# Fused attention and feed-forward on one core: weight loads issued back to back, a norm moved to another engine, and two groups of small steps re-timed

## The chip, the cores and the metric

The kernel runs on one NeuronCore of one Trainium2 chip. The metric is the device time of one execution in microseconds (us), as the median of several runs; lower is better. The profile is one execution taken by the hardware profiler; its span (279.4 us before the change) is about 2 us shorter than the measured time (281.28 us). Every run quoted is fast, with a granted TensorE clock of 0.997 to 1.0, unless the text says otherwise.

Engine names in the profile: PE is TensorE (matmuls), PEld its weight loads, DVE is VectorE, ACT is ScalarE, POOL is GpSimd, SP is SyncE. An added q (POOLq, SPq, PEq) is that engine's queue or sequencer.

## The reference, cut to what matters

For 8 batches, 8 heads, 576 tokens and head size 64, the first half is an attention without a score matrix: Q is normalised over the head size, K over the tokens, and K-transposed times V is a 64 by 64 matrix per head. The second half is a feed-forward layer on 4608 tokens of width 512, with 2048 hidden units and a swish that has its own `beta` per hidden unit.

```python
q_s = exp(q - max_d(q));  q_s = q_s / (sum_d(q_s) + 1e-9)
k_s = exp(k - max_s(k));  k_s = k_s / (sum_s(k_s) + 1e-9)
kv  = einsum('bhsd,bhse->bhde', k_s, v)
x   = einsum('bhsd,bhde->bhse', q_s, kv)      # then reshaped to [4608, 512]
h   = x @ w_in                                # [4608, 2048]
g   = h * sigmoid(beta * h)
out = g @ w_out                               # [4608, 512]
```

## The kernel before

The kernel works through nine slabs. Slabs 0 to 7 hold the first 512 tokens of batches 0 to 7; slab 8 holds the 64 tokens left over of each batch. Each slab has two passes on TensorE. Pass 1 is 64 matmuls of `x @ w_in` (16 tiles of 4), each tile followed by a Silu on ScalarE and a scaling on VectorE. Pass 2 is the product with `w_out`. From slab 1 on it is done with sums of quarters, seven products in place of eight, for which VectorE makes the sums (`GS`, `WSUM`). The attention of the next batch is threaded into the matmuls of the slab before it or of its own slab: small steps get a tick number, and one tick is one matmul of pass 1 (32/56 of a tick in the fast pass 2).

The attention of one batch has these steps: `exp` of Q and K on ScalarE; row-sum and reciprocal of the norm on VectorE; the norm's multiply on VectorE or GpSimd; a transpose of Q to `QT` (on TensorE in the first batches, by DMA later); a cast of V to `VB`; K-V products; a scaling by VectorE (`KVD`); an output product and its copy to `XT`, which is what pass 1 reads. Each group covers two heads, and there are four groups (`hp` 0 to 3) to a batch.

Each engine runs its own instructions in program order. Compute instructions on GpSimd are made to wait for one another by the scheduler. And the weights are loaded by DMAs that GpSimd issues (they also change float32 to bf16 on the way), so a DMA can only be issued when GpSimd gets to it in its program.

```python
def norm_main(b, hp0, n, eng=DVE):
    ...
    add(DVE, lambda e: e.tensor_reduce(s_, a, AX.X, ALU.add), r=ks, w=[("qs", i, hp0)])
    add(DVE, lambda e: e.reciprocal(v_, s_), r=[("qs", i, hp0)], w=[("qi", i, hp0)])
    add(eng, lambda e: e.tensor_tensor(a, a, vb, ALU.mult), r=ks + [("qi", i, hp0)], w=ks)
...
def norm_turn(b, hp0):            # norm of two groups, multiply on GpSimd, transpose by DMA
    norm_main(b, hp0, 2, POOL)
    turn(b, hp0, 2)
...
# the head of the program
norm_main(0, 0, 1, DVE)
norm_main(0, 1, 1, POOL)
load_win(0, 512, 0, 2)            # first piece of WIN, 256 KB in SBUF
norm_main(0, 2, 1, DVE)
cast_vr_s(0)                      # cast of the 64 left-over rows of V, on GpSimd
norm_main(0, 3, 1, POOL)
load_win(0, 512, 2, 4)            # second piece, 256 KB
for c0 in range(512, DFF, 512):
    load_win(c0, c0 + 512)        # third to fifth piece, 512 KB each
for c in range(4):
    load_wout(c)                  # four pieces of WOUT, 512 KB each
...
# batch 1, issued in slab 0: its queries are loaded once WOUT's first piece has landed
load_main("qf", qt_h, QF, 1, split=4, after=P.writer[("wout", 3, 0)])
...
w_sum(0, 0, 4); w_sum(2, 0, 4)
norm_main(1, 0, 1, DVE)
norm_main(1, 1, 1, POOL)
cast_vr_s(1)
w_sum(0, 4, 4); w_sum(2, 4, 4)
norm_main(1, 2, 1, DVE)
norm_main(1, 3, 1, DVE)
...
# slab 3: batch 3's last two output steps; pass 1 starts with 3 tiles, all of m = 0 first,
# then m = 1, m = 2, m = 3, where matmul m reads XT[m]
todo += [(1, steps(out_step, 3, 2)), (2.5, steps(out_step, 3, 3, MB, ACTE))]
...
# slabs 4 to 6: K-V products of batch b spread over ticks 8 to 36
s = spread(kv_steps(b, (0, 1)) + kv_steps(b, (2, 3)), 8, 36)
```

(The pieces stand in the order of the program; cuts are marked by three dots, and the comments are mine.)

The softmax here doesn't subtract the row's maximum and nothing guards it: scores larger than these inputs give would overflow.

Of the kernel before, what the change touches and what calls it, by code (L numbers as in the profile page):

```python
# [41 lines left out]
class Program:  # L42
# [12 lines left out]
    def add(self, eng, fn, r=(), w=(), bank=(), slot=None, after=(), war=False):  # L55
        op = Op(eng, fn, slot)
        op.pos = len(self.ops)
        deps = op.deps
        deps.extend(after)
        for k in r:  # L60
            deps.extend(self.writer.get(k, ()))
            self.readers.setdefault(k, []).append(op)
        for k in w:
            for d in self.readers.get(k, ()):
                if d is not op and (war or not self._same(d, op)):
                    deps.append(d)
            for d in self.writer.get(k, ()):
                if not self._same(d, op):
                    deps.append(d)
            self.readers[k] = []  # L70
            self.writer[k] = [op]
        for k in bank:
            t = self.touch.setdefault(k, {})
            for e, d in t.items():
                if e != eng:
                    deps.append(d)
            t[eng] = op
        if eng == POOL and slot is None:
            if self.pool is not None:
                deps.append(self.pool)  # L80
            self.pool = op
        self.ops.append(op)
        return op
# [71 lines left out]
def bass_efficient_attn_shen__then__act_swish_beta_kernel(  # L155
# [12 lines left out]
    with ExitStack() as es:  # L168
# [50 lines left out]
        MB = (5, 6, 7)  # L219

        P = Program()
        add = P.add
# [101 lines left out]
        def norm_main(b, hp0, n, eng=DVE):  # L324
            i = b % 2
            a = bass.AP(EQ[i], hp0 * 512, [[2048, 128], [64, 8 * n], [1, 64]])
            s_ = bass.AP(QS[i], hp0 * 8, [[32, 128], [1, 8 * n]])
            v_ = bass.AP(QI[i], hp0 * 8, [[32, 128], [1, 8 * n]])
            vb = bass.AP(QI[i], hp0 * 8, [[32, 128], [1, 8 * n], [0, 64]])
            ks = [("eq", i, hp) for hp in range(hp0, hp0 + n)]  # L330
            add(DVE, lambda e: e.tensor_reduce(s_, a, AX.X, ALU.add), r=ks, w=[("qs", i, hp0)])  # L331
            add(DVE, lambda e: e.reciprocal(v_, s_), r=[("qs", i, hp0)], w=[("qi", i, hp0)])  # L332
            add(eng, lambda e: e.tensor_tensor(a, a, vb, ALU.mult), r=ks + [("qi", i, hp0)],  # L333
                w=ks)
# [13 lines left out]
            add(eng, lambda e: (e.copy if eng == ACTE else e.tensor_copy)(o, a),  # L348
                r=[("vf", i, hp), ("vone", i)], w=[("vb", i, hp)], after=after)

        def cast_vr_s(b):
            o = bass.AP(VRS[b], 0, [[NHP * VW, 128], [VW, NHP], [1, 128]])
            a = bass.AP(VRF, 0, [[512, 128], [128, NHP], [1, 128]])
            add(POOL, lambda e: e.tensor_copy(o, a), r=[("vrf", 0), ("vrf", 1)], w=[("vrs", b)])

        def cast_vr(b, hs=(0, 1), after=()):
            pi = (b // 2) % 2
# [66 lines left out]
        def kv_steps(b, hps, pool=MB):  # L424
            i = b % 2
            st = {}

            def one(n, hp, j):
                if n == 0 and j == 0:
                    st["b"] = bank(pool)  # L430
                bk = st["b"]
                l, r_, ke, kv, ko = kv_rows(b, hp, j)
                mm(PS[bk][:, 256 * n:256 * n + 129], l, r_[:, 0:129], j == 0, j == 4,
                   r=ke + kv, w=[("ps", bk)], bk=bk)
                if n == len(hps) - 1 and j == 4:
                    c, k_ = hps[0], len(hps)
                    s_ = bass.AP(PS[bk], 128, [[512, 128], [256, k_]])
                    add(DVE, lambda e: e.reciprocal(RC[i][:, c:c + k_], s_),
                        r=[("ps", bk)], w=[("rc", i, h2) for h2 in hps], bank=[bk])
                    for m, h2 in enumerate(hps):  # L440
                        kvd(b, h2, bk, 256 * m)
            return [lambda n=n, hp=hp, j=j: one(n, hp, j) for n, hp in enumerate(hps)
                    for j in range(5)]
# [54 lines left out]
            turn_rem()  # L498

        def attn(b):  # L500
            s = spread(kv_steps(b, (0, 1)) + kv_steps(b, (2, 3)), 8, 36)
            x = []
            for hp in range(NHP):
                x += out_step(b, hp, MB, ACTE if hp % 2 else DVE)
            s += spread(x, 84, 108)
            return s
# [17 lines left out]
        def spread(steps, lo, hi):  # L524
            return [(lo + (hi - lo) * k / len(steps), s) for k, s in enumerate(steps)]
# [50 lines left out]
        norm_main(0, 0, 1, DVE)  # L576
        norm_main(0, 1, 1, POOL)
        load_win(0, 512, 0, 2)
        norm_main(0, 2, 1, DVE)
        cast_vr_s(0)  # L580
        norm_main(0, 3, 1, POOL)
        load_win(0, 512, 2, 4)
        for c0 in range(512, DFF, 512):
            load_win(c0, c0 + 512)
# [2 lines left out]
        ones_s(1)  # L587
        ones(1)
        ones(0)
        exp_kr_s(0)  # L590
        cast_v(0, 0, DVE)
        go(t_steps(0, (0,), HEAD, ACTE))
        exp_k(0, 0, 1)
        warm(7, 0)
        go(t_steps(0, (1,), HEAD, ACTE))
        exp_k(0, 1, 1)
        cast_v(0, 1, DVE)
        warm(4, 0)
        go(t_steps(0, (2,), HEAD, ACTE))
        exp_k(0, 2, 1)  # L600
        cast_v(0, 2, DVE)
        go(kv_steps(0, (0,), HEAD))
        warm(3, 0)
        go(t_steps(0, (3,), HEAD, ACTE))
        exp_k(0, 3, 1)
        go(kv_steps(0, (1,), HEAD))
        cast_v(0, 3, DVE)
        warm(2, 0)
        go(out_step(0, 0, HEAD, ACTE))
        go(kv_steps(0, (2,), HEAD))  # L610
        go(out_step(0, 1, HEAD, ACTE))
# [225 lines left out]
        for t in range(NSLAB):  # L837
            todo = []
            if t == 0:
                todo = [(x, steps(t_steps, 1, (hp,), NOW, ACTE))  # L840
                        for hp, x in enumerate((97, 106, 114, 119))]
                todo += [(107, one(exp_kr_s, 1))]
                todo += [(x, one(exp_k, 1, hp, 1)) for hp, x in enumerate((108, 115, 120, 125.5))]
                todo += [(x, one(cast_v, 1, hp, DVE if hp else POOL))
                         for hp, x in enumerate((115, 118.5, 123, 127))]
                todo += [(x, steps(kv_steps, 1, (hp,), NOW))
                         for hp, x in enumerate((118, 122, 126))]
                todo += [(x, steps(out_step, 1, hp, NOW, ACTE)) for hp, x in enumerate((121, 125))]
                todo += [(117, one(o2_evac, 0, 0, 3, ACTE))]
                todo += [(2, steps(out_step, 0, 3, HEAD, DVE))]  # L850
            elif t < 4:
                todo = attn_late(t + 1)
                if t == 3:
                    todo += [(1, steps(out_step, 3, 2)), (2.5, steps(out_step, 3, 3, MB, ACTE))]
                if t == 1:
                    todo += [(1, steps(out_step, 1, 2, (3,), ACTE)),
                             (3, steps(kv_steps, 1, (3,), (7,))),
                             (6, steps(out_step, 1, 3, (7,), DVE)),
                             (6.1, one(w_diff, 0)), (6.2, one(w_diff, 1))]
            elif t < 7:  # L860
                todo = attn(t + 1)
                if t > 3:
                    todo += spread(outr_steps(2 * t - 5), *((72, 88), (40, 56), (60, 76))[t - 4])
            elif t == 7:
                todo = spread(outr_steps(1), 32, 48)
# [74 lines left out]
            if t == 1:  # L940
                on(0, exps, 2)
                on(0, casts, 2)
                on(0, load, 4)
                on(2, norm_main, 2, 0, 2, POOL)
                on(3, norm_main, 2, 2, 2, POOL)
                on(3, g_diff, 0)
            elif t == 2:
                on(0, exps, 3)
                on(2, norm_turn, 3, 0)
                on(3, norm_turn, 3, 2)  # L950
                on(3, g_diff, 0)
                on(3, load, 5)
                on(4, exp_q, 4)
                on(4, casts, 4)
                on(6, norm_turn, 4, 0)
                on(7, norm_turn, 4, 2)
            elif t == 3:
                on(0, exp_k, 4)
                on(0, exp_kr, 4)
                on(0, exp_q, 5)  # L960
                on(3, g_diff, 0)
                on(4, norm_turn, 5, 0)
                on(5, norm_turn, 5, 2)
                on(4, exp_qr)
                on(5, exp_k, 5)
                on(5, norm_turn_rem)
                on(5, casts, 5)
                on(5, load, 6)
                on(7, load_rem, "qrf", qt_h, QRF, 4)
            elif t + 2 < B:  # L970
                b = t + 2
                on(0, exps, b)
                on(0, casts, b)
                if t == 4:
                    on(0, load, 7)
                on(3, norm_turn, b, 0)
                on(4, norm_turn, b, 2)
# [40 lines left out]
```

## Time and profile before

| | |
|---|---|
| time | 281.28 us (281.21 to 281.29, 3 runs) |
| span of the profiled run | 279.4 us |
| TensorE busy | 269.5 us, 96% |
| granted TensorE clock | 0.998 |

TensorE is busy 96% of the span, so a change to the other engines can only win what TensorE spends waiting. This is the line of the profile page with busy time, share of the span and number of instructions of each engine.

```profile
PE 269.5 (96%) x1844; PEld 167.7 (60%) x1844; DVE 192.6 (69%) x413; ACT 182.7 (65%) x285; POOL 65.2 (23%) x84
```

The view of waits for the kernel before tells who TensorE waited for. The columns are: engine and line of what waited, the engine and line (or DMA) that released it, then the idle us in total, the number of waits, and the longest one.

```profile
PE PS L376 <- DMA WIN<-in_moe_w_in_dram: 1.5, 2, 1.0
PE PS L376 <- POOL VB L348: 1.3, 1, 1.3
PE PS L376 <- DVE XT L456: 1.3, 1, 1.3
PE PS L376 <- DVE WARM L225: 1.2, 1, 1.2
```

The last of these is the start of the program. The other three are three separate places in time.

**The head.** The timeline of GpSimd before the change; the columns are start, us from the first start to the last end, engine, line, operation, output and input, count, and in brackets the idle time ahead.

```profile
9.40 0.95 POOL L551 DMA_DIRECT2D WIN<-in_moe_w_in_dram  x1
10.36 0.64 POOL L354 CAST VRS<-VRF 128x512 bf16<-128x512 f32 x1
11.08 1.10 POOL L333 TENSOR_TENSOR EQ<-EQ,QI 128x512 bf16<-128x512 bf16 x1
12.14 3.06 POOL L551 DMA_DIRECT2D WIN<-in_moe_w_in_dram  x4
15.16 2.99 POOL L557 DMA_DIRECT2D WOUT<-in_moe_w_out_dram  x4
```

A cast and a multiply stand between the first WIN issue and the other four. TensorE's timeline of the same kernel shows what comes of that: it starts on WIN at 14.87, stops at 16.61 for the second piece, and at 19.94 for the third.

```profile
15.58 1.03 PE L376 MATMUL PS<-XT,WIN 128*128 128x512 bf16 x4
17.61 2.33 PE L376 MATMUL PS<-XT,WIN 128*128 128x512 bf16 x10 [1.00 <-DMA WIN<-in_moe_w_in_dram]
20.42 10.53 PE L376 MATMUL PS<-XT,WIN 128*128 128x512 bf16 x48 [0.48 <-DMA WIN<-in_moe_w_in_dram]
```

The view of windows gives each engine's busy time (and number of instructions) for each microsecond; the last three columns are the granted clock, the DMA engines' busy share (it can exceed 1) and the GB/s that they moved.

```profile
15.00:16.00 1.00, 1.00 (x6) 0.31 (x4) 0.52 (x2) 0.91 (x2) 1.00 (x3) 1.00 0.79 85
16.00:17.00 1.00, 0.61 (x3) 0.10 (x1) 0.47 (x1) 0.99 (x2) 1.00 (x2) 1.00 0.89 127
```

From 18 us on the same column reads about 205 GB/s. So there is a hole in the weight stream just while TensorE waits for weights.

**Slab 3.** The timeline around 108 us, before the change: VectorE's row-sum and reciprocal for batch 4 are ahead of the third XT copy of batch 3, and TensorE stops for that copy.

```profile
107.41 1.21 DVE L331 TENSOR_REDUCE QS<-EQ 128x16 f32<-128x1024 bf16 x1
107.42 0.81 PE L376 MATMUL PS<-XT,WIN 128*128 128x512 bf16 x3
108.65 0.25 DVE L332 RECIPROCAL QI<-QS 128x16 f32<-128x16 f32 x1
108.82 0.63 DVE L456 CAST XT<-PS 128x512 bf16<-128x512 f32 x1
109.51 1.68 PE L376 MATMUL PS<-XT,WIN 128*128 128x512 bf16 x7 [1.28 <-DVE XT L456]
```

**Slab 4.** After eight matmuls of pass 1 comes the first K-V product of batch 5, and its V cast on GpSimd is not done.

```profile
136.40 1.89 PE L376 MATMUL PS<-XT,WIN 128*128 128x512 bf16 x8
138.92 2.65 POOL L348 CAST VB<-VF 128x512 bf16<-128x512 f32 x4
139.59 0.23 PE L376 MATMUL PS<-VB,EK 128*128 128x129 bf16 x1 [1.30 <-POOL VB L348]
```

### The profile page before, as it was taken

How to read it: one execution, taken by the hardware profiler on the slowest of the kernel's cores; microseconds unless marked ns; L12 is line 12 of the kernel's file. 1: busy time of each engine (PE TensorE's matmuls, PEld its weight loads, DVE VectorE, ACT ScalarE, POOL GpSimd, SP SyncE). 2: the span in 40 equal slices, each digit the busy share in tenths (PEclk: the TensorE clock that was granted, in tenths of full speed). 3: DMA queues.
4: the chain of work that ended last, by engine and by line, in shares of the span. 5: the costliest groups of instructions: out<-in, count | busy, mean ns of one | idle time of the engine just before them, and what ended most of it. 6: DMA issues, size and time to landing. Idle time of an engine off the chain costs nothing.

```text
span 279.4 us, 4714 instructions
## 1 busy us (share of the span) xinstructions
PE 269.5 (96%) x1844; PEld 167.7 (60%) x1844; DVE 192.6 (69%) x413; ACT 182.7 (65%) x285; POOL 65.2 (23%) x84
## 2 busy tenths in 40 slices
PE   8979999999999998999899999999999999999994
PEld 3434444448754784468555885488548844874583
DVE  4944586787758797768749794969487649635862
ACT  4777658789478965886677946794674467018610
POOL 2791021006521089000720551035100100000000
PEclk9999999999999999999999999999999999999999
DMA  7999999999992029920389999202700130003005
GB/s 214 314 163 206 223 320 350 290 244 371 360 256 118 0 49 286 305 116 0 65 258 297 328 339 165 95 4 51 231 2 0 21 150 0 2 26 124 2 0 150
DMA packets 57253, 45.39 MB, mean 162 GB/s; under 512 B 26496, under 2 KB 56208, under 8 KB 56208
## 3 DMA queue, kind: packets, MB, share of 16 engines
q1 hardware_dynamic: 52368, 40.38, 50.9%
q0 software_dynamic: 4240, 4.19, 9.3%
q10 hardware_dynamic: 624, 0.53, 0.6%
q8 instruction: 14, 0.23, 0.3%
q14 instruction: 7, 0.06, 0.1%
HBM read 36.71 MB, written 9.44 MB: 165 GB/s over the span
## 4 chain that ended last, share of the span: by engine, by line
PE 81%; DVE 8%; POOL 5%; DMA 3%; issue 1%; ACT 0%; POOLq 0%
PE PS L376 53%; PE PS L727 28%; POOL EQ L333 3%; DMA WIN<-in_moe_w_in_dram 3%; DVE QS L331 2%; DVE GT L693 1%; POOL VB L348 1%; PE PS L374 1%; DVE XT L456 1%; DVE KVD L418 1%; DVE QI L332 1%; DVE O2S L775 1%; POOL VR L361 0%; POOL EQR L341 0%; POOL WIN L551 0%
## 5 line engine op out<-in xcount | busy, mean ns | idle before, releaser
L376 PE MATMUL PS<-XT,WIN 128*128 128x512 bf16 x576 | 131.5, 379 | 2.8 <-DMA WIN<-in_moe_w_in_dram 1.5
L627 ACT ACTIVATE GT<-PS,BETA 128x512 bf16<-128x512 f32 x144 | 95.4, 689 | 43.3 <-PE PS L376 42.7
L376 PEld LDWEIGHTS PS<-XT,WIN 128*128 128x128 bf16 x576 | 53.5, 98 | 64.2 <-DMA WIN<-in_moe_w_in_dram 2.5
L650 DVE TENSOR_SCALAR GT<-GT,RB 128x512 bf16<-128x512 bf16 x144 | 51.0, 373 | 43.0 <-ACT GT L627 42.6
L333 POOL TENSOR_TENSOR EQ<-EQ,QI 128x1024 bf16<-128x1024 bf16 (+1 forms) x15 | 28.0, 1867 | 68.9 <-DVE QI L332 68.2
L727 PE MATMUL PS<-WOUT,GT 128*128 128x256 bf16 x256 | 33.6, 273 | 0.0
L727 PE MATMUL PS<-WSUM,GT 128*128 128x256 bf16 x256 | 31.9, 273 | 0.1
L727 PE MATMUL PS<-WOUT,GS 128*128 128x256 bf16 x256 | 30.4, 273 | 0.0
L727 PEld LDWEIGHTS PS<-WSUM,GT 128*128 128x128 bf16 x256 | 24.9, 98 | 4.0 <-issue 0.2
L727 PEld LDWEIGHTS PS<-WOUT,GT 128*128 128x128 bf16 x256 | 25.0, 98 | 3.4
L727 PEld LDWEIGHTS PS<-WOUT,GS 128*128 128x128 bf16 x256 | 24.6, 98 | 3.4
L763 ACT COPY O2S<-PS 128x512 f32<-128x512 f32 (+1 forms) x17 | 9.4, 561 | 24.1 <-PE PS L727 22.7
L300 ACT ACTIVATE EQ<-QF 128x512 bf16<-128x512 f32 x32 | 17.9, 619 | 6.9 <-DMA QF<-in_q_dram 6.9
L376 PE MATMUL PS<-VB,EK 128*128 128x129 bf16 x128 | 20.7, 220 | 1.7 <-POOL VB L348 1.3
L686 DVE TENSOR_TENSOR GS<-GT 128x512 bf16<-128x512 bf16 (+2 forms) x32 | 21.9, 684 | 0.0
L348 POOL CAST VB<-VF 128x512 bf16<-128x512 f32 x25 | 15.5, 620 | 26.1 <-DVE GS L686 14.9
L331 DVE TENSOR_REDUCE QS<-EQ 128x16 f32<-128x1024 bf16 (+1 forms) x20 | 19.8, 991 | 0.7 <-ACT EQ L300 0.7
L693 DVE TENSOR_TENSOR GT<-GT 128x2048 bf16<-128x2048 bf16 x16 | 19.6, 1251 | 0.0
L300 ACT ACTIVATE EK<-KF 128x512 bf16<-128x512 f32 x32 | 18.1, 619 | 0.0
L456 ACT CAST XT<-PS 128x512 bf16<-128x512 f32 x18 | 10.3, 582 | 10.0 <-PE PS L376 10.0
L775 DVE TENSOR_TENSOR O2S<-TS,PS 128x512 f32<-128x512 f32 (+1 forms) x17 | 10.7, 643 | 8.9 <-PE PS L727 8.9
L727 PE MATMUL PS<-WSUM,GS 128*128 128x256 bf16 x128 | 16.4, 273 | 0.0
(77 smaller groups left out, 241.2 us busy)
## 6 DMA issues: line engine op xcount, KB each, us to landing
out_dram<-O2S SPq DMA_DIRECT2D x8, 1024.0 KB, 4.9
QF<-in_q_dram SPq DMA_DIRECT2D x6, 1024.0 KB, 7.6
KF<-in_k_dram SPq DMA_DIRECT2D x6, 1024.0 KB, 9.4
VF<-in_v_dram SPq DMA_DIRECT2D x6, 1024.0 KB, 12.5
KF<-in_k_dram SPq DMA_DIRECT2D x8, 256.0 KB, 5.5
VF<-in_v_dram SPq DMA_DIRECT2D x8, 256.0 KB, 5.5
WOUT<-in_moe_w_out_dram POOLq DMA_DIRECT2D x4, 512.0 KB, 16.3
WIN<-in_moe_w_in_dram POOLq DMA_DIRECT2D x3, 512.0 KB, 9.2
```

The lines of the kernel that those rows point to most:

```text
L300: add(ACTE, lambda e, o=o, a=a: e.activation(o, a, ACT.Exp), r=[(name + "f", i, hp)], w=[("e" + name, i, hp)])
L331: add(DVE, lambda e: e.tensor_reduce(s_, a, AX.X, ALU.add), r=ks, w=[("qs", i, hp0)])
L333: add(eng, lambda e: e.tensor_tensor(a, a, vb, ALU.mult), r=ks + [("qi", i, hp0)], w=ks)
L348: add(eng, lambda e: (e.copy if eng == ACTE else e.tensor_copy)(o, a), r=[("vf", i, hp), ("vone", i)], w=[("vb", i, hp)], after=after)
L376: add(PE, lambda e: e.matmul(o, l, r_, start=start, stop=stop), r=r, w=w, bank=[bk])
L456: add(eng, lambda e: (e.copy if eng == ACTE else e.tensor_copy)(XT[i][:, hp, :], PS[bk][:, :]), r=[("ps", bk)], w=[("xt", i, hp)], bank=[bk])
L627: add(ACTE, lambda e: e.activation(GT[:, f, :], PS[bk][:, :], ACT.Silu, scale=BETA[:, f:f + 1]), r=[("ps", bk), "beta"], w=[("gt", f, 0), ...
L650: add(DVE, lambda e: e.tensor_scalar(GT[:, f, :], GT[:, f, :], RB[:, f:f + 1], None, ALU.mult), r=k + ["rb"], w=k)
L686: add(DVE, lambda e: e.tensor_tensor(GS2[:, i:i + n, :], GT[:, i:i + n, :], GT[:, i + NG:i + NG + n, :], ALU.add), r=[k_ for f in (i, i + ...
L693: add(DVE, lambda e: e.tensor_tensor(gv(f, th, NG), gv(f, th, NG), gv(f, 1 - th, NG), ALU.subtract), r=gk(f, 0, NG) + gk(f, 1, NG), w=gk(f ...
L727: add(PE, lambda e, l=l, r_=r_, st=st, u=u, i=i, b_=b_: e.matmul(PS[b_][:, 256 * u:256 * u + 256], l, r_, start=st, stop=end and i == NG - ...
L775: add(DVE, lambda e, b_=b_, u0=u0, u1=u1: e.tensor_tensor(o[:, u0:u1, :], ts[:, u0:u1, :], bank3(b_)[:, u0:u1, :], ALU.add), r=["ts", ("ps ...
```

## The change

The intent is to close these three gaps. In the head, GpSimd keeps only one norm multiply and then issues all nine weight DMAs; the VRS cast goes to ScalarE, the other multiply to VectorE, where it and the V casts get a new order, and three warm-up matmuls (filler on zeros) are dropped. In slab 3, the third XT copy goes to ScalarE and the fourth to VectorE, and batch 4's second norm moves behind them. In slab 4, the K-V products of batch 5 start 10 ticks later.

```diff
-        def cast_vr_s(b):
+        def cast_vr_s(b, eng=POOL):
...
-            s = spread(kv_steps(b, (0, 1)) + kv_steps(b, (2, 3)), 8, 36)
+            s = spread(kv_steps(b, (0, 1)) + kv_steps(b, (2, 3)), *((18, 46) if b == 5 else (8, 36)))
...
         norm_main(0, 1, 1, POOL)
         load_win(0, 512, 0, 2)
-        norm_main(0, 2, 1, DVE)
-        cast_vr_s(0)
-        norm_main(0, 3, 1, POOL)
         load_win(0, 512, 2, 4)
...
+        norm_main(0, 2, 1, DVE)
         exp_kr_s(0)
         cast_v(0, 0, DVE)
         go(t_steps(0, (0,), HEAD, ACTE))
         exp_k(0, 0, 1)
+        cast_vr_s(0, ACTE)
         warm(7, 0)
         go(t_steps(0, (1,), HEAD, ACTE))
         exp_k(0, 1, 1)
+        warm(2, 0)
+        go(t_steps(0, (2,), HEAD, ACTE))
+        norm_main(0, 3, 1, DVE)
         cast_v(0, 1, DVE)
-        warm(4, 0)
-        go(t_steps(0, (2,), HEAD, ACTE))
         exp_k(0, 2, 1)
-        cast_v(0, 2, DVE)
         go(kv_steps(0, (0,), HEAD))
         warm(3, 0)
+        cast_v(0, 2, DVE)
...
-        warm(2, 0)
+        warm(1, 0)
...
-                    todo += [(1, steps(out_step, 3, 2)), (2.5, steps(out_step, 3, 3, MB, ACTE))]
+                    todo += [(1, steps(out_step, 3, 2, MB, ACTE)), (2.5, steps(out_step, 3, 3)),
+                             (4, one(norm_turn, 4, 2))]
...
                 on(6, norm_turn, 4, 0)
-                on(7, norm_turn, 4, 2)
```

More of the change, by code (lines that the diff above doesn't have):

```diff
@@ L349, in cast_v @@
                 r=[("vf", i, hp), ("vone", i)], w=[("vb", i, hp)], after=after)
-        def cast_vr_s(b):
+        def cast_vr_s(b, eng=POOL):
             o = bass.AP(VRS[b], 0, [[NHP * VW, 128], [VW, NHP], [1, 128]])
             a = bass.AP(VRF, 0, [[512, 128], [128, NHP], [1, 128]])
-            add(POOL, lambda e: e.tensor_copy(o, a), r=[("vrf", 0), ("vrf", 1)], w=[("vrs", b)])
+            add(eng, lambda e: (e.copy if eng == ACTE else e.tensor_copy)(o, a),
+                r=[("vrf", 0), ("vrf", 1)], w=[("vrs", b)])
         def cast_vr(b, hs=(0, 1), after=()):
```

## The prediction

> **What bounds the kernel.** 281.28 us, span 279.4. TensorE is the limit: the page gives PE 269.5 us busy (96%) at full granted clock, and the chain that ended last is 81% PE. Only closing PE idle gaps can win. The waits of PE name few: weights WIN by DMA 1.5 us (2 waits), XT copies by VectorE 1.28 (once), VB casts by GpSimd 1.30 (once). In order of time:
>
> 1. Head. The timeline shows GpSimd issuing WIN's first piece at 9.40, then a VRS cast (0.64) and a second norm multiply (1.10), and only from 12.14 the next four pieces (0.76 each). They land about 14.5, 17.6, 20.3, 22.9, 25.8 (DMA view). PE waits 1.00 us until 17.61 and 0.48 until 20.42, then never again for WIN. From 14 to 17 us the DMA engines move only 85 to 132 GB/s against 205 afterwards: the late issue leaves a hole.
> 2. Slab 3. At 109.51 PE resumes after 1.28 us: batch 3's third XT copy sat on VectorE behind batch 4's second row-sum (1.21) and reciprocal (0.25).
> 3. Slab 4. At 139.59 PE resumes after 1.30 us: batch 5's first K-V product waits for its VB cast on GpSimd, done about 139.55.
>
> **What the change does.**
>
> 1. The VRS cast goes to ScalarE (about 0.6) and the norm multiply to VectorE (0.69), so WIN's second to fifth pieces are issued from about 10.35, 1.8 us earlier. The hole is some 320 KB deep, 1.6 us at 205 GB/s (estimate): the third piece should land near 18.7 instead of 20.3. VectorE gets 0.69 more in a full stretch, but its three V casts took 2.04 us while GpSimd multiplied, against 0.42 each elsewhere. The Trainium skill ("SBUF — State Buffer", Terms: the port pair that VectorE and GpSimd share) says that the loser blocks; the longest cast, 1.26 us, agrees. So the last XT copy should still end near 16.5, the 16 leading matmuls near 18.6. Saving 1.6 us (0.9 to 2.2): both waits and little more. WOUT's earlier landings pull batch 1's loads forward as much.
> 2. ScalarE, idle 2.24 us there, takes the third copy (0.59); VectorE does the fourth ahead of the row-sum. Both are ready when PE reaches them (108.1 and 108.7). Saving 1.28. Batch 4's second GpSimd multiply was queued behind the first until 110.3 anyway.
> 3. The K-V products start 10 matmuls (2.16 us) later: PE arrives at 138.29 + 2.16 = 140.45, 0.9 us after the cast; later casts come every 0.66 us, faster than PE asks. Saving 1.30.
>
> The three gaps lie on the chain in sequence, so they add. What follows is PE bound or triggered by PE and moves along.
>
> **Prediction.** 281.28 - 1.6 - 1.3 - 1.3 = 277.1 us, 8 in 10 between 276.2 and 278.6. Faster by over 2% (under 275.7): 0.04; within 2%: 0.95; slower: 0.01.
>
> **Right or wrong.** Right: five WIN issues in a row from 9.4; PE steady from about 18.7 instead of 20.42; no PE waits for XT by VectorE near 108 or VB by GpSimd near 137; span about 275.2. Wrong: a PE wait at the fourth batch-0 transpose for VectorE's multiply, or a head XT copy after 17.5, giving part of the head's gain back.
>
> **What would make it wrong.** WIN's earlier descriptors delay the last K and V loads and so the head's attention; VectorE's casts and GpSimd's descriptor writing block each other; the closed gaps had hidden another wait behind them (ScalarE's table load before the first Silu, 1.28).

## The result, and the profile after

| | before | after |
|---|---|---|
| time, median | 281.28 us (281.21 to 281.45, 4 runs) | 277.15 us (277.07 to 277.23, 4 runs) |
| ratio after to before | | 0.9852, 95% interval 0.9835 to 0.9869 |
| span of the profiled run | 279.4 us | 275.2 us |
| TensorE busy | 269.5 us, 96% | 269.1 us, 98% |

A ratio here is the mean time of one kernel's fast runs over the mean time of the other's fast runs of the same rounds, so it is not quite the ratio of the medians. The change is 4.13 us, 1.5%, clear of noise, and inside the 2% band.

Busy time of the engines after the change, and TensorE's waits, in the same columns as before. The lines of the program are one further down now, so L376 has become L377.

```profile
PE 269.1 (98%) x1841; PEld 167.9 (61%) x1841; DVE 193.8 (70%) x414; ACT 183.1 (67%) x286; POOL 64.0 (23%) x82
```

```profile
PE PS L377 <- DVE WARM L225: 1.2, 1, 1.2
PE PS L375 <- POOL EQ L333: 0.7, 2, 0.5
PE PS L375 <- DVE EQ L333: 0.4, 1, 0.4
```

All three waits are gone. Two small ones that were 0.2 or nothing are there instead, both at transposes (L375).

The head after the change, on GpSimd, on TensorE, and then by windows:

```profile
9.41 4.16 POOL L552 DMA_DIRECT2D WIN<-in_moe_w_in_dram  x5
13.55 3.03 POOL L558 DMA_DIRECT2D WOUT<-in_moe_w_out_dram  x4
```

```profile
15.32 0.39 PE L377 MATMUL PS<-QT,KVD 128*128 128x512 bf16 x1
15.54 6.74 PE L377 MATMUL PS<-XT,WIN 128*128 128x512 bf16 x30
```

```profile
15.00:16.00 1.00, 1.00 (x6) 0.33 (x5) 0.52 (x2) 0.98 (x2) 1.00 (x3) 1.00 1.24 205
16.00:17.00 1.00, 1.00 (x6) 0.47 (x5) 0.43 (x1) 0.99 (x2) 0.89 (x4) 1.00 1.25 209
```

The five WIN issues stand in a row, the hole in the stream is filled to 205 to 209 GB/s, and TensorE runs through without idle time. Its last attention product of the head starts at 15.32, against 15.36 before: the head's attention has not become faster, only the weights are there in time. The seventeenth WIN matmul, the first that needs the third piece, starts at 18.65; before it was 20.42. That is 1.77 us. Counted from 15.54 in matmul spacings of 0.216 us it could have started at 18.57, so the third piece, which lands at 11.08 + 7.53 = 18.60, still holds TensorE for 0.08 us. The record of the matmul ahead lasts until 18.73, so no idle time of TensorE shows; the line of its weight loads shows the wait (the 0.41 is idle time of the weight loads, not of TensorE):

```profile
18.65 3.35 PEld L377 LDWEIGHTS PS<-XT,WIN 128*128 128x128 bf16 x17 [0.41 <-DMA WIN<-in_moe_w_in_dram]
```

Slab 3 after the change: both copies come ahead of the row-sum, and TensorE does not stop.

```profile
105.68 0.59 ACT L457 CAST XT<-PS 128x512 bf16<-128x512 f32 x1 [1.59 <-PE PS L377]
106.12 6.21 PE L377 MATMUL PS<-XT,WIN 128*128 128x512 bf16 x28
106.33 0.69 DVE L457 CAST XT<-PS 128x512 bf16<-128x512 f32 x1
106.93 1.21 DVE L331 TENSOR_REDUCE QS<-EQ 128x16 f32<-128x1024 bf16 x1
```

Slab 4 after the change: 18 matmuls instead of 8 come before the first K-V product, which then finds its cast done.

```profile
133.65 4.05 PE L377 MATMUL PS<-XT,WIN 128*128 128x512 bf16 x18
137.54 0.22 PE L377 MATMUL PS<-VB,EK 128*128 128x129 bf16 x1
```

**Where the time came from.** The same matmul can be looked up in both traces, and the difference of its start times is what has been gained up to there.

| matmul | before | after | gained so far |
|---|---|---|---|
| seventeenth WIN matmul, slab 0 | 20.42 | 18.65 | 1.77 |
| first transpose of batch 1 (slab 0, pass 2) | 37.92 | 36.14 | 1.78 |
| second transpose of batch 1 | 40.26 | 38.96 | 1.30 |
| slab 3, three matmuls ahead of the XT gap | 107.42 | 106.12 | 1.30 |
| slab 4, first matmul | 136.40 | 133.65 | 2.75 |
| last VectorE operation of the program | 275.79 | 271.56 | 4.23 |

So the head gives 1.77 at first (the expectations of e1 and e5 say 1.85, which was counted in spacings and leaves out the hold of 0.08) and 1.30 in the end; slab 3 gives 2.75 - 1.30 = 1.45; slab 4 gives 4.23 - 2.75 = 1.48. (The medians differ by 4.13; the two profiled runs by 4.2 in span.) The half microsecond that the head loses again goes at one spot, the second transpose of batch 1. These lines of the timeline are TensorE's first two transposes there, first before and then after the change.

```profile
37.92 0.39 PE L374 MATMUL PS<-IDB,EQ 128*128 128x128 bf16 x4
40.26 0.40 PE L374 MATMUL PS<-IDB,EQ 128*128 128x128 bf16 x4
```

```profile
36.14 0.39 PE L375 MATMUL PS<-IDB,EQ 128*128 128x128 bf16 x4
38.96 0.40 PE L375 MATMUL PS<-IDB,EQ 128*128 128x128 bf16 x4 [0.49 <-POOL EQ L333]
```

Batch 1's queries are loaded, in quarters, when WOUT's first piece has landed. From issue times and landing times that was 15.16 + 13.2 = 28.4 us before and 13.55 + 13.4 = 26.95 after: the DMA stream moved by 1.4 us, TensorE by 1.77. The `exp` that is released by the second quarter of the queries moved by 1.30, as its lines show, first before and then after:

```profile
37.16 0.63 ACT L300 ACTIVATE EQ<-QF 128x512 bf16<-128x512 f32 x1 [1.89 <-DMA QF<-in_q_dram]
```

```profile
35.86 0.63 ACT L300 ACTIVATE EQ<-QF 128x512 bf16<-128x512 f32 x1 [2.03 <-DMA QF<-in_q_dram]
```

In both kernels the row-sum and GpSimd's multiply (1.31 us in both) follow, and the second transpose starts 0.06 us after that multiply ends. So the second transpose starts when this chain lets it. That was so before the change too: the matmul ahead of it starts at 39.87 and the transpose at 40.26, which is 0.18 us more than the spacing of 0.216. The head's net gain is therefore what the query loads moved, 1.30 us, and not the two waits for WIN that were closed: by these traces, closing those alone would have gained nothing beyond this spot. The profile of e3 below, whose head is that of the kernel before, agrees: its seventeenth WIN matmul starts 0.18 us later (20.60), and its second transpose at 40.26 again. No run moves WIN's issues without WOUT's, so this split is read from the traces and not tested by itself.

Note also that a gap costs more than its idle time. The XT gap reads 1.28 us idle, but the matmuls ahead of it start at 107.42 and three spacings of 0.216 end at 108.07; TensorE goes on at 109.51, so 1.44 us of starts are lost. The record of a matmul is 0.379 us long where the next one can start after 0.216; the rest of the last one, 0.16 us, counts as busy.

### The profile page after: what moved, and what is told of

The parts are those of the page before. It is cut to its first block, busy times and chain, and to the rows that moved or that the text cites. A ratio compares the mean times of both kernels' runs of the same rounds, so it can differ in the third digit from the quotient of the medians.

```text
span 275.2 us, 4707 instructions
## 1 busy us (share of the span) xinstructions
PE 269.1 (98%) x1841; PEld 167.9 (61%) x1841; DVE 193.8 (70%) x414; ACT 183.1 (67%) x286; POOL 64.0 (23%) x82
## 4 chain that ended last, share of the span: by engine, by line
PE 83%; DMA 8%; POOL 4%; DVE 2%; issue 1%; ACT 0%; SPq 0%; POOLq 0%
PE PS L377 49%; PE PS L728 33%; DMA WOUT<-in_moe_w_out_dram 5%; DMA QF<-in_q_dram 3%; POOL EQ L333 2%; POOL WIN L552 1%; POOL VB L348 1%; PE PS L375 1%; DVE QS L331 1%; POOL VR L362 0%; DVE XT L457 0%; ACT GT L628 0%; DVE EQ L333 0%; DVE QI L332 0%; ACT EQ L300 0%
## 5 line engine op out<-in xcount | busy, mean ns | idle before, releaser
L377 PE MATMUL PS<-XT,WIN 128*128 128x512 bf16 x576 | 131.0, 379 | 0.1
L377 PEld LDWEIGHTS PS<-XT,WIN 128*128 128x128 bf16 x576 | 53.6, 98 | 61.1 <-DVE XT L457 0.6
L651 DVE TENSOR_SCALAR GT<-GT,RB 128x512 bf16<-128x512 bf16 x144 | 52.1, 381 | 37.1 <-ACT GT L628 36.4
L333 POOL TENSOR_TENSOR EQ<-EQ,QI 128x1024 bf16<-128x1024 bf16 (+1 forms) x14 | 26.9, 1921 | 66.9 <-DVE QI L332 66.2
L377 PE MATMUL PS<-VB,EK 128*128 128x129 bf16 x128 | 20.6, 220 | 0.0
```

The lines of the kernel that those rows point to most:

```text
L377: add(PE, lambda e: e.matmul(o, l, r_, start=start, stop=stop), r=r, w=w, bank=[bk])
L651: add(DVE, lambda e: e.tensor_scalar(GT[:, f, :], GT[:, f, :], RB[:, f:f + 1], None, ALU.mult), r=k + ["rb"], w=k)
```

## The experiments

Twelve kernels ran, in three groups, each group on one chip with its own nine runs of the kernel before (medians 281.18, 281.29 and 281.28 us). The kernel after was not run again in these groups; a difference to it is one to its 277.15 us of the main result. All gave correct results.

### Group 1: each part by itself, and the issue time by itself

**e1, the head alone** (the change without its edits to slabs 3 and 4):

```diff
         load_win(0, 512, 0, 2)
-        norm_main(0, 2, 1, DVE)
-        cast_vr_s(0)
-        norm_main(0, 3, 1, POOL)
         load_win(0, 512, 2, 4)
 ... (and the other edits of the head, as shown above)
```

> Only the head's part (WIN issued back to back, VRS cast on ScalarE, batch 0's last norm multiply on VectorE, three warm-ups fewer) on the kernel before. My theory, read from the two traces: 1.3 us of the 4.13 come from here (PE gains 1.85 at its seventeenth WIN matmul and gives 0.5 back at batch 1's second transpose), so about 279.95 us. The prediction on record said 1.6, so 279.7. PE waits for XT (slab 3) and VB (slab 4) stay at about 1.28 and 1.30. Rival: the parts lean on one another and the head alone gains nothing, because the later gaps grow: about 281.3.

Measured: 280.11 us (ratio 0.9961, 0.9949 to 0.9974), 1.07 us below the kernel before. In the trace the second transpose of batch 1 starts at 38.96, against 40.26, so 1.30 there, and the waits for XT and VB are unchanged. This is less than the 1.6 of the prediction and the rival (nothing gained) is out.

**e2, slab 3 alone:**

```diff
-todo += [(1, steps(out_step, 3, 2)), (2.5, steps(out_step, 3, 3, MB, ACTE))]
+todo += [(1, steps(out_step, 3, 2, MB, ACTE)), (2.5, steps(out_step, 3, 3)),
+         (4, one(norm_turn, 4, 2))]
 on(6, norm_turn, 4, 0)
-on(7, norm_turn, 4, 2)
```

> Only batch 3's copies and batch 4's second norm moved, on the kernel before. My theory: the wait for XT goes, 1.44 us in matmul starts (idle 1.28 plus 0.16 of overlap that an idle gap costs), so about 279.85 us; the other waits stay. Rival: the wait moves on to a later matmul (fourth copy or ScalarE's table load) and less than half is gained: 280.6 or more.

Measured: 279.93 us (0.9953, 0.9939 to 0.9967), 1.25 us gained. The XT wait is gone from TensorE's waits; VB still stands at 1.3.

**e3, slab 4 alone:**

```diff
-spread(kv_steps(b, (0, 1)) + kv_steps(b, (2, 3)), 8, 36)
+spread(kv_steps(b, (0, 1)) + kv_steps(b, (2, 3)), *((18, 46) if b == 5 else (8, 36)))
```

> Only batch 5's K-V products 10 matmuls later, on the kernel before. My theory: the wait for VB goes, 1.47 us in matmul starts, so about 279.8 us. Rival: the postponed VectorE work (KVD) and output steps meet later and give part of it back: over 280.3.

Measured: 279.73 us (0.9947, 0.9935 to 0.996), 1.45 us gained. The VB wait is gone, XT stays at 1.3.

The three parts by themselves gain 1.07 + 1.25 + 1.45 = 3.8 us, and together 4.13. The intervals of the single ratios are about 0.36 us wide to each side, so the parts add up within what these runs resolve.

**e4, the kernel after with late WIN issues.** GpSimd has memsets to do that stand behind the weight DMAs. Putting some of them between the first and the second WIN piece delays the issues without any new work and without a change to the other engines' programs.

```diff
         load_win(0, 512, 0, 2)
+        ones_s(1)
+        ones(1)
         load_win(0, 512, 2, 4)
 ...
-        ones_s(1)
-        ones(1)
         ones(0)
```

> The kernel after, with GpSimd's memsets of ones_s(1) and ones(1) (about 2.2 us in a row, work it does anyway, only later) put between the first and the second WIN piece; VectorE's, ScalarE's and PE's programs are as in the kernel after. My theory (the time of issue of WIN's later pieces makes the head's gain): second piece issued near 12.6, PE waits for WIN come back (together 1.5 to 2.3 us), total 278.6 to 279.1. Rival (the gain comes from the shorter chain of casts and fewer warm-ups, whatever GpSimd does): within 0.3 of 277.15.

Measured: 278.85 us (0.9917, 0.9903 to 0.9931), 1.7 us above the kernel after. The second piece is issued at 12.40, and TensorE's two waits for WIN are back, as its timeline shows:

```profile
17.04 2.33 PE L377 MATMUL PS<-XT,WIN 128*128 128x512 bf16 x10 [0.36 <-DMA WIN<-in_moe_w_in_dram]
20.59 3.63 PE L377 MATMUL PS<-XT,WIN 128*128 128x512 bf16 x16 [1.23 <-DMA WIN<-in_moe_w_in_dram]
```

So with the head's casts and norms as in the kernel after, and only the issues late, the gain of the head is gone: the second transpose of batch 1 starts at 40.34, against 40.26 before the change. It is the issue time that makes it, and not a shorter chain of casts or fewer warm-ups. The edit delays WOUT's issues too (the first from 13.55 to 15.34), so it does not tell WIN's part from WOUT's.

### Group 2: why each part works, by doses

**e5, batch 1's queries loaded earlier:**

```diff
-load_main("qf", qt_h, QF, 1, split=4, after=P.writer[("wout", 3, 0)])
+load_main("qf", qt_h, QF, 1, split=4, after=P.writer[("win", 12, 0)])
```

> The kernel after, with batch 1's query loads let go when WIN's last piece has landed, one 512 KB piece (about 2.6 us) before WOUT's first piece. My theory: of PE's 1.85 us in the head 0.5 is given back at batch 1's second transpose (near 38.9 us), because its queries wait for the stream of weight pieces, which the change moved by only 1.4 us; so that wait (0.49 idle) goes and the time falls by 0.5 to 0.65, to about 276.6. Rival: the wait is GpSimd's slow multiply (1.31 us) or the DMA engines are full anyway and the wait only moves to WOUT: no gain, 277.0 or more.

Measured: 278.54 us (0.9898, 0.9883 to 0.9913), 1.4 us slower than the kernel after. The expectation failed. The queries came earlier (the first `exp` at 31.12 instead of 33.20), but the WOUT pieces that VectorE needs came later (its two sums start at 34.66 instead of 32.82), and VectorE's program has a sum of WOUT quarters ahead of batch 1's first row-sum. This is the timeline of that run around the first transpose:

```profile
31.12 0.63 ACT L300 ACTIVATE EQ<-QF 128x512 bf16<-128x512 f32 x1
34.66 1.29 DVE L706 TENSOR_TENSOR WSUM<-WOUT 128x1024 bf16<-128x1024 bf16 x2 [2.34 <-DMA WOUT<-in_moe_w_out_dram]
35.87 0.68 DVE L331 TENSOR_REDUCE QS<-EQ 128x8 f32<-128x512 bf16 x1
37.57 0.40 PE L375 MATMUL PS<-IDB,EQ 128*128 128x128 bf16 x4 [1.36 <-DVE EQ L333]
```

VectorE stands idle 2.34 us for WOUT while the first `exp` of the queries has long been done, and TensorE then waits 1.36 us where it did not wait before. This fits a limited stream, in which what one load gains another loses; VectorE's order ties the norms to WOUT as well. Group 3 starts from there.

**e6, slab 3 with the norm moved and the copies on their old engines:**

```diff
-todo += [(1, steps(out_step, 3, 2)), (2.5, steps(out_step, 3, 3, MB, ACTE))]
+todo += [(1, steps(out_step, 3, 2)), (2.5, steps(out_step, 3, 3, MB, ACTE)),
+         (4, one(norm_turn, 4, 2))]
 on(6, norm_turn, 4, 0)
-on(7, norm_turn, 4, 2)
```

> On the kernel before, only batch 4's second norm moved behind batch 3's copies; the copies keep their engines. My theory: VectorE's row-sum ahead of the third copy is the whole cause, so nearly all of batch 3's gain comes with this alone: the XT wait falls from 1.28 to under 0.15, time about 279.9. Rival: ScalarE taking the third copy is what matters: less than 0.7 gained here.

Measured: 279.97 us (0.9957, 0.9945 to 0.997), 1.32 us gained, as much as both edits together in e2 (one of its five runs took 280.81, the others 279.81 to 280.05); no XT wait is left in TensorE's waits.

**e7, slab 3 with only the engines swapped:**

```diff
-todo += [(1, steps(out_step, 3, 2)), (2.5, steps(out_step, 3, 3, MB, ACTE))]
+todo += [(1, steps(out_step, 3, 2, MB, ACTE)), (2.5, steps(out_step, 3, 3))]
```

> On the kernel before, only the engines of batch 3's last two copies swapped; the norm stays ahead. My theory: now the fourth copy waits behind the row-sum and comes at the same time as the third did, but PE needs it 3 matmuls (0.65 us) later: half of the gain, time about 280.5, a wait for XT of about 0.6. Rival: the swap is what matters: about 279.9.

Measured: 280.83 us (0.9978, 0.9966 to 0.9991), 0.46 us gained, 0.79 in its profiled run (280.5 us). The wait has moved to the fourth copy and shrunk to 0.63, as its timeline shows:

```profile
108.78 0.63 DVE L456 CAST XT<-PS 128x512 bf16<-128x512 f32 x1
109.46 1.90 PE L376 MATMUL PS<-XT,WIN 128*128 128x512 bf16 x8 [0.63 <-DVE XT L456]
```

VectorE's copy still ends at the same time, only TensorE needs the fourth one three matmuls later than the third. So the cause of the gap is the row-sum ahead of the copy in VectorE's program; moving that alone is enough, and the swap of engines adds nothing that these runs can resolve.

**e8, the kernel after with the K-V products put off by 4 ticks instead of 10:**

```diff
-*((18, 46) if b == 5 else (8, 36))
+*((12, 40) if b == 5 else (8, 36))
```

> The kernel after, with batch 5's K-V products 4 matmuls later than in the kernel before instead of 10. My theory: the wait for VB shrinks by what the products are put off, 4 times 0.216 = 0.86 of 1.47 us, so PE waits about 0.45 idle and the time is about 0.6 above the kernel after, 277.75. Rival: any spreading away from the start of the slab is enough: 277.15.

Measured: 277.71 us (0.9872, 0.9859 to 0.9886), 0.56 us above the kernel after, with this line on TensorE:

```profile
136.62 0.23 PE L377 MATMUL PS<-VB,EK 128*128 128x129 bf16 x1 [0.43 <-POOL VB L348]
```

The wait shrinks from 1.30 to 0.43, by 0.87 us, where the products were put off by 4 x 0.216 = 0.86. Nothing later in the program took the gain back.

### Group 3: the half microsecond that the head gave back

**e9, the three warm-ups put back:**

```diff
-        warm(2, 0)      # ahead of batch 0's third transpose
+        warm(4, 0)
...
-        warm(1, 0)      # ahead of batch 0's first output product
+        warm(2, 0)
```

> The kernel after with the three dropped warm-up matmuls put back (two before batch 0's third transpose, one before its first output product). My theory: they are filler that fits in PE's idle time in the head, so within 0.3 us of 277.15. Rival: the shorter head program is a good part of its gain: three matmuls of 0.216 us, so about 0.65 slower, 277.8.

Measured: 277.16 us (0.9859, 0.9846 to 0.9873), the same as the kernel after. A wait for XT of 0.3 us appears in TensorE's waits, but the second transpose of batch 1 starts at 39.02, against 38.96, although the seventeenth WIN matmul of this run starts at 18.38 and not at 18.65: what TensorE gains or loses ahead of that spot does not count as long as it still waits there for the query chain (0.61 us in this run).

**e10, batch 1's second norm multiply on VectorE:**

```diff
-norm_main(1, 1, 1, POOL)
+norm_main(1, 1, 1, DVE)
```

> The kernel after with batch 1's second norm multiply on VectorE (0.69) instead of GpSimd (1.31). The run with the earlier query load showed that VectorE's program order, weight sums ahead of norms, counts here, not the loads alone. Theory: the wait at the second transpose (0.49) goes, but the third transpose then meets its own multiply, which is behind the two weight sums (2.09) on VectorE: wait about 0.4 there, gain 0 to 0.3.

Measured: 277.17 us (0.9859, 0.9845 to 0.9872), no gain. The second transpose (38.21) starts without a wait. The third one (40.90) waits instead, for a multiply that stands behind the two weight sums in VectorE's program:

```profile
38.00 1.28 DVE L706 TENSOR_TENSOR WSUM<-WOUT 128x1024 bf16<-128x1024 bf16 x2
38.21 0.39 PE L375 MATMUL PS<-IDB,EQ 128*128 128x128 bf16 x4
40.90 0.40 PE L375 MATMUL PS<-IDB,EQ 128*128 128x128 bf16 x4 [0.57 <-DVE EQ L333]
```

**e11, the same, and two weight sums moved out of the way** (they are needed only in slab 1's second pass):

```diff
-norm_main(1, 1, 1, POOL)
+norm_main(1, 1, 1, DVE)
 cast_vr_s(1)
-w_sum(0, 4, 4)
-w_sum(2, 4, 4)
 ...
-(6.1, one(w_diff, 0)), (6.2, one(w_diff, 1))]
+(6.03, one(w_sum, 0, 4, 4)), (6.06, one(w_sum, 2, 4, 4)),
+(6.1, one(w_diff, 0)), (6.2, one(w_diff, 1))]
```

> As the run before, and the last two of the first weight sums moved from between batch 1's norms to the start of slab 1. Theory: no wait of PE at any of batch 1's transposes; 0.5 to 0.65 us less than the kernel after: 276.5 to 276.65; ratio to the kernel before 0.983. Rival: the sums then push VectorE's scaling in slab 1 so far that PE waits at slab 1's second pass: no gain.

Measured: 276.91 us (276.71 to 276.92, 5 runs; ratio 0.9848, 0.9835 to 0.9861). That is 0.25 us below e9 and e10 of the same group, half of what was expected. The transposes of batch 1 no longer wait, but the first K-V product of batch 1 does, for its V cast on GpSimd:

```profile
40.66 1.14 POOL L348 CAST VB<-VF 128x512 bf16<-128x512 f32 x1 [0.43 <-DMA VF<-in_v_dram]
41.85 0.40 PE L377 MATMUL PS<-VB,EK 128*128 128x129 bf16 x4 [0.38 <-POOL VB L348]
```

That cast is released by the load of V, so it hangs on the same DMA stream, and it took 1.14 us where the median of the casts on GpSimd in that run is 0.613.

**e12, only the weight sums moved, the multiply left on GpSimd:** the second half of e11's edit.

```diff
-w_sum(0, 4, 4)
-w_sum(2, 4, 4)
 ...
+(6.03, one(w_sum, 0, 4, 4)), (6.06, one(w_sum, 2, 4, 4)),
```

> The kernel after with only those two weight sums moved; the multiply stays on GpSimd. If the 1.31 us of that multiply come from meeting VectorE's two-input weight sum (it took 1.04 when they did not overlap fully), it falls to about 1.0 and PE's wait at the second transpose from 0.49 to about 0.2: 276.8. If not, the multiply stays at 1.3 and the time at 277.15.

Measured: four runs of 276.66 to 276.79 us, and one of 726.45 us, which is left out (ratio of the fast runs 0.9843, 0.983 to 0.9857). The profile is of the slow execution. In it TensorE's WIN matmuls start 0.621 us apart (median), against 0.216 in the kernel after, although the granted clock reads 1.0; VectorE's scalings keep their length (0.353 us, against 0.352). What slowed TensorE is open. The multiply took 1.04 us there, with no weight sum beside it, against 1.31: that part of the expectation is borne out, as far as a slow execution can show it. How much shorter TensorE's wait gets at full speed is in no trace. By times this kernel has the lowest median (its fast runs overlap those of e11), 0.4 us below the kernel after: its four fast runs and those of e9 and e10 in the same group (277.11 to 277.31) do not overlap. The intervals of the ratios to the kernel before do overlap with the kernel after's, so the size of this last gain is less certain than its sign.

## Why the prediction was right or wrong

The total was right: 277.1 us was predicted, 277.15 measured, with the span at 275.2 as foretold. Point by point:

- **TensorE bound, three gaps in sequence that add.** Right. Each gap closed by itself in e1 to e3, the gains sum to 3.8 against 4.13 together, and TensorE's busy time hardly changed (269.5 to 269.1 us).
- **Head: earlier issues close both waits for WIN.** Right in mechanism. The five issues stand in a row from 9.41, and from issue and landing time the third piece lands at 11.1 + 7.5 = 18.6, where 18.7 was predicted. The first matmul after the 16 leading ones starts at 18.65, where 18.6 was predicted. Late issues alone bring the waits back (e4). But the closed waits are not what is left of the gain in the end, as the next point shows.
- **Head: 1.6 us saved, and "WOUT's earlier landings pull batch 1's loads forward as much".** This step failed. TensorE gained 1.77 us at its seventeenth WIN matmul, more than the prediction's 1.6, but WOUT's first landing moved by 1.4 only and the second quarter of batch 1's queries by 1.30, and at batch 1's second transpose TensorE waits 0.49 us for the chain that starts there. The head's net gain is 1.30 us. e11 shows how tied this is: with the transposes' waits gone, the V cast, released by a load, becomes the next wait.
- **Slabs 3 and 4: 1.28 and 1.30 saved.** The mechanism was right and the terms were too small: 1.45 and 1.48 in the traces, because the idle time leaves out 0.16 us of the matmul ahead of it. These two terms were 0.35 us too small together, and the head's term 0.3 us too large (1.6 against 1.30), so the errors nearly cancel: the close hit of the total is in part luck.
- **Slab 3: "ScalarE takes the third copy; VectorE does the fourth ahead of the row-sum".** Right as a sum, but the two edits are not equal: moving the norm does it alone (e6), the swap alone leaves a wait of 0.63 us (e7).
- **Slab 4: the wait shrinks by what the products are put off.** Right, by the dose in e8 (0.56 us lost where about 0.6 was expected).
- **VectorE has room in the head because its casts get shorter.** Right in the main: the four casts took 0.64, 0.42, 0.42 and 0.42 us, and the last XT copy starts at 15.74, as at 15.78 before. The prediction named a wait at the fourth batch-0 transpose for VectorE's multiply as a sign of failure. That wait came (0.37 us) and cost nothing by the end of the head, since TensorE's last attention product there was not later than before. As a sign it was chosen badly.
- **A hidden wait behind the gaps.** The prediction looked for it at ScalarE's table load before the first Silu; TensorE's waits after the change name none there. It was at batch 1's second transpose in slab 0.

The experiment e5 was a wrong step: it took "the loads are late" for the whole cause, and overlooked that VectorE's program put sums that need WOUT ahead of the norms.

## What to carry to other kernels

When one engine is busy 96% of the time, list its waits, find the moment of each, and look for the instruction that stands in front of the releaser in that engine's program: here each of three gaps was a question of order and not of work. A DMA that an engine issues behind compute is as late as that compute, and the hole in the stream's GB/s shows it. After a stream has been moved forward, compare how far the stream moved with how far the busy engine moved: the smaller of the two is what is kept when the two meet again.

## What the Trainium skill lacked or had wrong

- "SBUF — State Buffer", Who interferes with whom, says that a VectorE instruction with two SBUF inputs contends with a GpSimd instruction that reads SBUF. Two weight sums took 2.09 us where they met GpSimd's multiply (kernel after) and 1.28 us where they did not (e10), and a V cast on GpSimd took 1.14 us beside VectorE's norm multiply, against 0.613 as the median (e11). The page gives no such durations for these pairs.
- "SBUF — State Buffer", the box on VectorE blocking DMAs that GpSimd issues: this case shows little of such harm. Five WIN issues took 4.16 us in a row with three of VectorE's float32 casts beside them (kernel after), against 0.95 + 3.06 = 4.01 us for the same five before, with two casts beside them. No run here takes the casts away, and none shows that these casts run in the mode that the box speaks of.
- "DMA: Bandwidth & Descriptors", Anatomy of one DMA, gives a fit of 2.0 us plus bytes over 436e3 for one DMA from GpSimd, so about 2.6 us for 256 KB (an estimate from the page). Here the 256 KB pieces of WIN took 5.1 and 5.4 us beside other loads, and a queue of such pieces, which also change float32 to bf16, moved about 205 GB/s counted in bf16. The page has no figure for pieces that cast, nor for a queue beside other traffic.
- "Trainium Kernel Development and Optimization", Performance Expectations, calls matmul busy time a bad metric for how close a kernel is to roofline, because matmuls are pipelined. It lacks the consequence for gaps: an idle time read from the trace is too small by the overlap, here 0.379 - 0.216 = 0.16 us for each gap behind a matmul of 512 columns, and a shorter hold shows no idle time at all (0.08 us at 18.65 in the kernel after).
